# A last output tile split 384 to 128 and copied out by two engines, six more stores, and the k-v products of batch two copied out first

## The chip, the cores and the metric

One core of a Trainium2 chip. The metric is the device time of one execution in microseconds (us); a kernel's runs agree within some tenths of a us here, and all runs compared below are of the fast state (granted TensorE clock 0.996 to 1.000 in the profiled ones). Runs of one call stand beside runs of the kernel before on the same chip.

## The reference, cut to what matters

```python
    # attention: q, k, v of shape (8, 8, 576, 64), float32
    def phi(x, c, s):
        r = np.maximum(x, 0.0)
        return np.concatenate([r * c, r * s], axis=-1)
    q_p = phi(q, cos_w, sin_w)
    k_p = phi(k, cos_w, sin_w)
    kv = np.einsum('bhsf,bhsd->bhfd', k_p, v)
    z = np.sum(k_p, axis=2)
    num = np.einsum('bhsf,bhfd->bhsd', q_p, kv)
    den = np.einsum('bhsf,bhf->bhs', q_p, z)[..., None] + 1e-06
    return (num / den).astype(np.float32)
    # ... cut: the result, as x of 4608 tokens x 512, goes into the feed-forward layer, d_ff = 1536
    g = x @ w_gate
    silu = g * (1.0 / (1.0 + np.exp(-g)))
    val = x @ w_val
    return (silu * val @ w_out).astype(np.float32)
```

The products of the feed-forward layer (L513 and L549 in the profile) carry 86% of the chain that ended last.

## The kernel before

Everything is scheduled by hand: engines run their instructions in the order in which the program names them, and a framework inserts the semaphore waits. TensorE writes its products to PSUM ("banks" in the profile); ScalarE and VectorE copy them out of it, and SyncE issues most of the stores. The parts that matter are the copies of batch two's k-v products and of its turned (transposed) q from PSUM, and the output tiles.

```python
def qturn_pe(b, j, lo, hi, eng):          # transposes of q on TensorE, then one copy ("phit")
    ps = take(1)...
    for c in range(lo, hi):
        nc.tensor.transpose(out=ps[:, c - lo], in_=st["qp"][:, b, c, j], identity=ident)   # L274
    copy_op(eng, qt_of(b)[...], ps[...])                                                   # L333

def kv_out(b, engs=("act", "dve"), js=slice(0, J)):     # four copies ("kvd"), two per engine
    ps = st[b, "kvps"]
    for e, eng in enumerate(engs):                      # e: one bank per engine
        for i in range(2):
            (nc.scalar.copy if eng == "act" else nc.vector.tensor_copy)(out=kvd[b % 2]..., in_=ps[hs, e, ...])  # L297
# ... cuts ...
def ffn_out(t, f0=0, f1=None):            # one tile of 128 rows x 512 columns
    ...                                   # 12 products into one bank (L549)
    ob = obp.tile([P, d_model], FP32, name="ob")
    (nc.scalar.copy if t % 2 == 0 else nc.vector.tensor_copy)(out=ob, in_=ps)
    for e in range(2):
        idx = 2 * t + e
        nc.sync.dma_start(out=out_v[idx // NC, idx % NC], in_=ob[e * SH:(e + 1) * SH])

def ffn_out_last(t):                      # the last tile, in two column parts
    for lo, hi in ((0, 320), (320, d_model)):
        ps = take(1)[:, 0:hi - lo]
        for fc in range(FC):
            nc.tensor.matmul(out=ps, lhsT=hts[tg % 2][:, fc, r:r + P], rhs=wo_sb[:, fc, lo:hi], ...)   # L568
        ob = obp.tile([P, d_model], FP32, name="ob")
        nc.scalar.copy(out=ob[:, 0:hi - lo], in_=ps)                                                    # L571
        for e in range(2):
            idx = 2 * t + e
            (nc.sync if e else nc.scalar).dma_start(out=out_v[...][:, lo:hi], in_=ob[e * SH:(e + 1) * SH, 0:hi - lo])
# ... cuts ...
at("b11", lambda: kv_mm(1), q_(1, 0, 0), q_(1, 1, 0, "dve"), lambda: kv_out(1))
```

Stores issued by SyncE and ScalarE take eight completion counters in turn, 0 to 7. At the end of the program SyncE waits for the counters one by one, in the order 0 to 7.

Of the kernel before, what the change touches and what calls it, by code (L numbers as in the profile page):

```python
# [18 lines left out]
def kernel(  # L19
# [10 lines left out]
    nc = tc.nc  # L30
# [4 lines left out]
    SH = 64  # L35
    NC = S // SH
    d_model, d_ff = moe_w_gate.shape
# [4 lines left out]
    NH = B * NC  # L42
# [23 lines left out]
    def take(n, hold=None):  # L66

        taken = {x for r in held.values() for x in r}
        free = [b for b in range(0, 8, n) if not any(b <= x < b + n for x in taken)]

        b0 = min(free, key=lambda b: (n == 1 and hold is not None and hold[0] == "o" and b ^ 1 not in taken,
                                      sorted(used[b:b + n], reverse=True)))
        if hold is not None:
            held[hold] = range(b0, b0 + n)
        touch(range(b0, b0 + n))
        return banks[:, b0] if n == 1 else banks[:, b0:b0 + n]
# [6 lines left out]
    def give_back(hold):  # L83
        touch(held.pop(hold))
# [64 lines left out]
    def idle_products(n, cols=P):  # L149
# [37 lines left out]
        out=tab.rearrange("p c e d -> p (c e) d"),  # L187
        in_=csk.rearrange("p c e -> p (c e)").to_broadcast([P, NC * 2, D]),
# [74 lines left out]
    def relu_slots(b, lo, hi, js=slice(0, J), eng="dve"):  # L263

        if "qp" not in st:
            both = rel.tile([P, G, NC, 2, D], BF16, name="r_q").rearrange("p g c w d -> p (g c w d)")
            st["qp"] = both.rearrange("p (b c j x) -> p b c j x", b=2, c=NC, j=J)
        relu_op(eng, st["qp"][:, b, lo:hi, js].rearrange("p c j (i d) -> p c (j i) d", i=2),
                raws[b, "q"][:, 2 * js.start:2 * js.stop, lo:hi].rearrange("p g c d -> p c g d"))

    def qturn_pe(b, j, lo, hi, eng):
        ps = take(1).bitcast(BF16).rearrange("p (c x) -> p c x", x=P)
        for c in range(lo, hi):
            nc.tensor.transpose(out=ps[:, c - lo], in_=st["qp"][:, b, c, j], identity=ident)  # L274
        copy_op(eng, qt_of(b)[:, :, j, lo:hi].rearrange("p e c s -> p c e s"),
                ps[:, 0:hi - lo].rearrange("p c (e s) -> p c e s", e=2))

    def kv_mm(b):
        ps = st[b, "kvps"] = take(2, ("kv", b))
        for j, c in [(j, c) for j in range(J) for c in range(NC)]:  # L280
            for i in range(2):
                for e in range(2):
                    es = slice(e * SH, (e + 1) * SH)
                    g = 2 * j + i
                    nc.tensor.matmul(  # L285
                        out=ps[i * D:(i + 1) * D, e, j * 2 * D1:(j + 1) * 2 * D1],
                        lhsT=raws[b, "k"][es, g, c],
                        rhs=v2s[b % 2][es, g, c, :, 0:D1],
                        start=(c == 0), stop=(c == NC - 1),
                    )  # L290

    def kv_out(b, engs=("act", "dve"), js=slice(0, J)):
        ps = st[b, "kvps"]
        for e, eng in enumerate(engs):
            for i in range(2):
                hs = slice(i * D, (i + 1) * D)
                (nc.scalar.copy if eng == "act" else nc.vector.tensor_copy)(  # L297
                    out=kvd[b % 2][hs, e, js, :, i].rearrange("p j w x -> p (j w) x"),
                    in_=ps[hs, e, js.start * 2 * D1:js.stop * 2 * D1].rearrange("p (y x) -> p y x", x=D1))
# [10 lines left out]
    def kv_free(b):  # L310
        give_back(("kv", b))
# [226 lines left out]
    out_v = out.rearrange("(b p c) f -> b c p f", p=SH, c=NC)  # L538
    o_ps = {}

    def ffn_out(t, f0=0, f1=None):

        f1 = FC if f1 is None else f1
        if f0 == 0:
            o_ps[t] = take(1, ("o", t))
        tg, i = divmod(t, GH // 2)
        r = i * P
        for fc in range(f0, f1):
            nc.tensor.matmul(out=o_ps[t], lhsT=hts[tg % 2][:, fc, r:r + P], rhs=wo_sb[:, fc],  # L549
                             start=(fc == 0), stop=(fc == FC - 1))  # L550
        if f1 < FC:
            return
        ps = o_ps.pop(t)
        give_back(("o", t))
        ob = obp.tile([P, d_model], FP32, name="ob")
        (nc.scalar.copy if t % 2 == 0 else nc.vector.tensor_copy)(out=ob, in_=ps)  # L556
        for e in range(2):
            idx = 2 * t + e
            nc.sync.dma_start(out=out_v[idx // NC, idx % NC], in_=ob[e * SH:(e + 1) * SH])

    def ffn_out_last(t):

        tg, i = divmod(t, GH // 2)
        r = i * P
        for lo, hi in ((0, 320), (320, d_model)):
            ps = take(1)[:, 0:hi - lo]
            for fc in range(FC):
                nc.tensor.matmul(out=ps, lhsT=hts[tg % 2][:, fc, r:r + P], rhs=wo_sb[:, fc, lo:hi],  # L568
                                 start=(fc == 0), stop=(fc == FC - 1))
            ob = obp.tile([P, d_model], FP32, name="ob")  # L570
            nc.scalar.copy(out=ob[:, 0:hi - lo], in_=ps)  # L571
            for e in range(2):
                idx = 2 * t + e
                (nc.sync if e else nc.scalar).dma_start(out=out_v[idx // NC, idx % NC][:, lo:hi],
                                                        in_=ob[e * SH:(e + 1) * SH, 0:hi - lo])


# [29 lines left out]
    def at(s, *fns):  # L607
        plan.setdefault(s, []).extend(fns)
# [5 lines left out]
    def a_(t, j):  # L614
        return lambda: (a_half(t, j), x_norm(t) if j else None)
# [4 lines left out]
    def q_(b, j, part, eng="act"):  # L620
        lo, hi = ((0, CUT), (CUT, NC))[part]
        return lambda: qturn_pe(b, j, lo, hi, eng)
# [72 lines left out]
    for g, s in enumerate(("b9", "b9", "b10", "b10")):  # L695
        at(s, lambda g=g: vmul(1, g))
    at("b10", lambda: relu_slots(1, 0, CUT, slice(0, 1), "act"), lambda: relu_slots(1, 0, CUT, slice(1, 2)))
    at("b11", lambda: kv_mm(1), q_(1, 0, 0), q_(1, 1, 0, "dve"), lambda: kv_out(1))
    at((0, 0), lambda: kv_free(1), a_(4, 0), a_(4, 1))
    at((0, 2), a_(5, 0))  # L700
    at((0, 3), a_(5, 1))
# [21 lines left out]
    for i, (piece, t) in enumerate(steps0):  # L723
        ffn_out(t, 4 * piece, 4 * piece + 4)
        slot(divmod(i, 4))
# [38 lines left out]
    for t in range(2 * OUT, NTG * OUT):  # L764
        tg, i = divmod(t, OUT)
# [12 lines left out]
    for tg in range(1, NTG):  # L778
        s0 = SLOTS * tg
        for fc in range(FC):  # L780
            ffn_fc(tg, fc)
            slot(s0 + fc)
        for i in range(OUT):
            if tg == NTG - 1 and i == OUT - 1:
                ffn_out_last(tg * OUT + i)
            else:
                ffn_out(tg * OUT + i)
            slot(s0 + FC + i)
# [31 lines left out]
```

## Time and profile before

| what | value |
|---|---|
| median of 3 runs | 325.12 us (324.85 to 325.15) |
| span in the profile | 323.2 us |
| TensorE busy | 316.1 us, 98% |
| last product's end to the end of the span (the "tail" below) | 3.985 us |
| batch two's first k-v product to the return to the output products | 4.139 us |

A line of the chain of waits has a start, a duration and what the chain passed through. In a line of groups or of the timeline stand the engine, the source line of the kernel, the operation, its output and inputs, and the number of elements; "[1.04 <-PE banks L568]" is idle time before it and what ended it.

### The profile page before, as it was taken

To read this page: it belongs to the slowest core of one execution; us is meant where nothing else is said; L and a number is where in the kernel's file an instruction comes from. 1 tells how busy PE (TensorE), PEld (TensorE's weight loads), DVE (VectorE), ACT (ScalarE), POOL (GpSimd) and SP (SyncE) were. 2 spreads that over 40 slices of the span, in tenths; PEclk is the share of its full clock that TensorE was granted. 3 is DMA by queue.
4 is the path that set the end of the run, shared out by engine and by line. 5 is a ranking of instruction groups with operands and counts; after the bars stand their busy time and mean duration, and the time that the engine had idled before them with its cause. 6 is when DMAs were issued, how large, how long until landed. Compare 5 with 4: busy or idle time off the path is not lost.

```text
span 323.2 us, 6031 instructions
## 1 busy us (share of the span) xinstructions
PE 316.1 (98%) x2384; PEld 159.0 (49%) x2384; DVE 180.9 (56%) x363; ACT 130.7 (40%) x239; POOL 35.3 (11%) x60
## 2 busy tenths in 40 slices
PE   7899999999999999999999999999999999999995
PEld 3596555454445444544454445444544444444443
DVE  7873766787448747564756555755573236323320
ACT  7553546662436345333533354335432132213311
POOL 6755002010101000110011000200000000000000
PEclk9999999999999999999999999999999999999999
DMA  7999997987995988599679968895912401240014
GB/s 267 215 200 197 206 194 136 213 113 108 178 200 79 184 152 134 79 175 177 116 97 160 164 123 118 134 184 109 134 36 48 103 14 35 50 103 11 0 32 97
DMA packets 74379, 41.01 MB, mean 127 GB/s; under 512 B 49904, under 2 KB 69104, under 8 KB 74352
## 3 DMA queue, kind: packets, MB, share of 16 engines
q1 hardware_dynamic: 52000, 22.95, 38.9%
q0 software_dynamic: 22192, 17.57, 36.6%
q8 instruction: 18, 0.29, 0.4%
q10 hardware_dynamic: 160, 0.13, 0.1%
q14 instruction: 9, 0.07, 0.1%
HBM read 37.75 MB, written 9.44 MB: 146 GB/s over the span
## 4 chain that ended last, share of the span: by engine, by line
PE 95%; ACT 2%; DVE 2%; issue 0%; ACTq 0%
PE banks L513 58%; PE banks L549 28%; PE banks L285 3%; PE banks L399 2%; PE banks L444 1%; PE banks L381 1%; DVE v L239 1%; PE banks L152 1%; PE banks L568 1%; PE banks L325 0%; PE banks L485 0%; ACT L184 0%; ACT phit L333 0%; PE banks L274 0%; ACT ob L571 0%; DVE qwT L369 0%
## 5 line engine op out<-in xcount | busy, mean ns | idle before, releaser
L524 DVE TENSOR_TENSOR ht<-sg,banks 128x512 bf16<-128x512 bf16 (+2 forms) x116 | 74.7, 650 | 68.7 <-PE banks L513 60.3
L513 PE MATMUL banks<-xT,wv_sb 128*128 128x512 bf16 (+2 forms) x464 | 111.3, 364 | 0.0
L513 PE MATMUL banks<-xT,wg_sb 128*128 128x512 bf16 (+2 forms) x464 | 111.3, 364 | 0.0
L519 ACT ACTIVATE sg<-banks 128x512 bf16<-128x512 f32 (+2 forms) x116 | 65.8, 568 | 111.6 <-PE banks L513 107.7
L549 PE MATMUL banks<-wo_sb,ht 128*128 128x512 bf16 x420 | 93.8, 379 | 0.0
L513 PEld LDWEIGHTS <-wv_sb 128*128 128x128 bf16 x464 | 44.8, 98 | 48.7
L513 PEld LDWEIGHTS <-wg_sb 128*128 128x128 bf16 x464 | 43.1, 98 | 42.8
L549 PEld LDWEIGHTS <-ht 128*128 128x128 bf16 x420 | 40.3, 98 | 45.7 <-issue 0.2
L556 ACT COPY ob<-banks 128x512 f32<-128x512 f32 x18 | 10.6, 586 | 54.0 <-PE banks L549 54.0
L235 DVE TENSOR_TENSOR r_q<-raw_q,tab 128x1152 bf16<-128x1152 bf16 x24 | 17.9, 754 | 20.7 <-ACT raw_q L218 20.7
L556 DVE COPY ob<-banks 128x512 f32<-128x512 f32 x17 | 11.7, 691 | 28.6 <-PE banks L549 28.6
L239 DVE TENSOR_TENSOR v<-raw_v,tab 128x1152 bf16<-128x1152 bf16 x31 | 22.8, 753 | 0.1
L421 DVE TENSOR_TENSOR x<-banks,rec 128x512 bf16<-128x512 f32 (+1 forms) x32 | 21.6, 674 | 1.3 <-PE banks L381 0.3
L218 ACT ACTIVATE raw_k<-raw_k 128x576 bf16<-128x576 bf16 (+1 forms) x25 | 17.1, 694 | 0.0
L218 ACT ACTIVATE raw_q<-raw_q 128x576 bf16<-128x576 bf16 x24 | 15.5, 679 | 0.0
L729 POOL COPY hold<-phit 1x2 bf16<-1x2 bf16 x5 | 0.9, 175 | 129.6 <-DMA phit<-r_q 129.6
L399 PEld LDWEIGHTS <-phit 128*128 128x128 bf16 (+1 forms) x240 | 10.0, 100 | 6.5 <-issue 1.3
L399 PE MATMUL banks<-kv,phit 128*128 128x65 bf16 (+1 forms) x240 | 11.6, 195 | 0.0
L152 PE MATMUL banks<-zeros 128*128 128x64 bf16 (+1 forms) x64 | 8.5, 292 | 1.0 <-DVE zeros L147 1.0
L308 DVE CAST kv<-banks 64x260 bf16<-64x260 f32 x12 | 5.1, 428 | 7.4 <-ACT kv L308 7.3
L285 PEld LDWEIGHTS <-raw_k 64*64 64x64 bf16 x504 | 7.6, 106 | 3.0 <-issue 2.1
L285 PE MATMUL banks<-v,raw_k 64*64 64x130 bf16 x504 | 8.8, 218 | 0.0
(84 smaller groups left out, 130.9 us busy)
## 6 DMA issues: line engine op xcount, KB each, us to landing
out_dram<-ob SPq DMA_DIRECT2D x70, 128.0 KB, 2.4
raw_k<-in_k_dram POOLq DMA_DIRECT2D x7, 576.0 KB, 9.1
raw_q<-in_q_dram POOLq DMA_DIRECT2D x6, 576.0 KB, 6.3
raw_v<-in_v_dram POOLq DMA_DIRECT2D x6, 576.0 KB, 12.0
wo_sb<-in_moe_w_out_dram POOLq DMA_DIRECT2D x3, 512.0 KB, 13.0
wg_sb<-in_moe_w_gate_dram POOLq DMA_DIRECT2D x5, 256.0 KB, 8.6
wv_sb<-in_moe_w_val_dram POOLq DMA_DIRECT2D x5, 256.0 KB, 9.2
wo_sb<-in_v_dram SPq DMA_DIRECT2D x2, 576.0 KB, 4.3
```

What stands on the lines that cost most here:

```text
L152: nc.tensor.matmul(out=ps, lhsT=zeros, rhs=zeros[:, 0:cols].unsqueeze(1).to_broadcast([P, 4, cols]), start=True, stop=True)
L218: nc.scalar.activation(out=out, in_=in_, func=AF.Relu)
L235: nc.vector.tensor_tensor(out=st[b, "q"][:, g], in0=o.unsqueeze(2).to_broadcast([P, NC, 2, D]), in1=tab, op=ALU.mult)
L239: nc.vector.tensor_tensor(out=v2s[b % 2][:, g, :, :, 0:D], in0=(first if b == 0 and g == 0 else {"v": raw_of(b, "v")})["v"][:, g].unsqueez ...
L285: nc.tensor.matmul(out=ps[i * D:(i + 1) * D, e, j * 2 * D1:(j + 1) * 2 * D1], lhsT=raws[b, "k"][es, g, c], rhs=v2s[b % 2][es, g, c, :, 0:D ...
L399: nc.tensor.matmul(out=ps[ms, e, g * D1:(g + 1) * D1], lhsT=phit[b][:, e, g, c:c + n].rearrange("p c s -> p (c s)"), rhs=kv2s[b % 2][:, e, ...
L421: nc.vector.tensor_tensor(out=st["x", t].rearrange("p (y e d) -> p e y d", e=2, d=D)[:, :, ys], in0=ps[:, :, 0:2 * J * D1].rearrange("p e ...
L513: nc.tensor.matmul(out=st["f", tg, fc, lo][i], lhsT=(wg_sb, wv_sb)[i][:, kc, fs], rhs=xT[tg][:, ts, kc], start=(kc == 0), stop=(kc == KC - 1))
L519: nc.scalar.activation(out=sg[:, 0:n], in_=st["f", tg, fc, lo][0], func=AF.Silu)
L524: nc.vector.tensor_tensor(out=hts[tg % 2][:, fc, r:r + n], in0=st.pop(("s", tg, fc, lo))[:, 0:n], in1=ps[1], op=ALU.mult)
L549: nc.tensor.matmul(out=o_ps[t], lhsT=hts[tg % 2][:, fc, r:r + P], rhs=wo_sb[:, fc], start=(fc == 0), stop=(fc == FC - 1))
L556: (nc.scalar.copy if t % 2 == 0 else nc.vector.tensor_copy)(out=ob, in_=ps)
```

## The change

Its intent, as far as the diff tells: to empty the k-v products as soon as they are there; to have less left after TensorE's last product and two engines on it; and, with six more stores, to give the last stores other completion counters.

```diff
@@ ffn_out
         for e in range(2):
             idx = 2 * t + e
-            nc.sync.dma_start(out=out_v[idx // NC, idx % NC], in_=ob[e * SH:(e + 1) * SH])
+            parts = 2 if NH - 10 <= idx < NH - 4 else 1
+            for i in range(parts):
+                cols = slice(i * d_model // parts, (i + 1) * d_model // parts)
+                nc.sync.dma_start(out=out_v[idx // NC, idx % NC][:, cols], in_=ob[e * SH:(e + 1) * SH, cols])
@@ ffn_out_last
-        for lo, hi in ((0, 320), (320, d_model)):
+        for lo, hi in ((0, 384), (384, d_model)):
...
-            nc.scalar.copy(out=ob[:, 0:hi - lo], in_=ps)
+            mid = (hi - lo) // 2
+            nc.scalar.copy(out=ob[:, 0:mid], in_=ps[:, 0:mid])
+            nc.vector.tensor_copy(out=ob[:, mid:hi - lo], in_=ps[:, mid:hi - lo])
             for e in range(2):
                 idx = 2 * t + e
-                (nc.sync if e else nc.scalar).dma_start(...)
+                (nc.scalar if e else nc.sync).dma_start(...)
@@ the plan
-    at("b11", lambda: kv_mm(1), q_(1, 0, 0), q_(1, 1, 0, "dve"), lambda: kv_out(1))
+    at("b11", lambda: kv_mm(1), lambda: kv_out(1), q_(1, 0, 0), q_(1, 1, 0, "dve"))
```

More of the change, by code (lines that the diff above doesn't have):

```diff
@@ L570, in ffn_out_last @@
             ob = obp.tile([P, d_model], FP32, name="ob")
-            nc.scalar.copy(out=ob[:, 0:hi - lo], in_=ps)
+            mid = (hi - lo) // 2
+            nc.scalar.copy(out=ob[:, 0:mid], in_=ps[:, 0:mid])
+            nc.vector.tensor_copy(out=ob[:, mid:hi - lo], in_=ps[:, mid:hi - lo])
             for e in range(2):
                 idx = 2 * t + e
-                (nc.sync if e else nc.scalar).dma_start(out=out_v[idx // NC, idx % NC][:, lo:hi],
+                (nc.scalar if e else nc.sync).dma_start(out=out_v[idx // NC, idx % NC][:, lo:hi],
                                                         in_=ob[e * SH:(e + 1) * SH, 0:hi - lo])
```

## The prediction

> **What bounds the kernel now.** I read four views in this order: the page's busy shares and chain, TensorE's gaps, the chain of waits around 38 to 46 us, and the records of the last 6 us.
>
> ```profile
> PE 316.1 (98%) x2384; PEld 159.0 (49%) x2384; DVE 180.9 (56%) x363; ACT 130.7 (40%) x239; POOL 35.3 (11%) x60
> ...
> PE 95%; ACT 2%; DVE 2%; issue 0%; ACTq 0%
> ```
>
> TensorE is busy 98% of the 323.2 us and carries 95% of the chain that ended last. So time is lost or won only where TensorE stands still, and after its last product. I compared each matmul's start with that of the one before. From 43 us to 319 us nothing but steps of 0.10 us is lost, 18 of them, each where products of one size or shape give way to another. Nothing waits for a load or a transpose there, so a shift of TensorE at 43 us should arrive whole at the end. One real stop lies just ahead, in the chain between 38 and 46 us (start us, us, what):
>
> ```profile
> 38.88 1.27 PE banks L285 x69
> 40.15 0.51 PE banks L274 x7
> 40.66 0.02 issue
> 40.69 0.91 ACT phit L333
> 41.59 0.27 ACT kvd L297
> 41.87 0.01 issue
> 41.88 0.38 ACT kvd L297
> 42.26 0.04 issue
> 42.30 0.72 PE banks L444 x7
> ```
>
> Batch two's k-v products end at 40.15. ScalarE then waits for the transposes of q, copies those out (phit), and only then copies the k-v products (kvd), although these were there first. TensorE comes to the attention products (L444) at 41.83, does one, and stands until 42.30: 0.36 us beyond its pace, ended by ScalarE's second kvd copy. VectorE's second one, ending at 42.48, costs another 0.12 us at 42.53. Together 0.48 us.
>
> The other place is the end. ScalarE's timeline from 317.9 us on, and the last stores (KB each, us from issue to landing):
>
> ```profile
> 318.26 0.43 ACT L571 COPY ob<-banks 128x320 f32<-128x320 f32 x1 [1.04 <-PE banks L568]
> 318.72 0.56 ACTq L574 DMA_DIRECT2D out_dram<-ob  x1
> 319.40 0.32 ACT L571 COPY ob<-banks 128x192 f32<-128x192 f32 x1 [0.71 <-PE banks L568]
> 319.75 0.50 ACTq L574 DMA_DIRECT2D out_dram<-ob  x1
> ```
>
> ```profile
> out_dram<-ob SPq DMA_DIRECT2D x1, 48.0 KB, 1.9
> out_dram<-ob ACTq DMA_DIRECT2D x1, 48.0 KB, 2.1
> ```
>
> TensorE's last product ends at 319.22, the last copy at 319.72, the last stores are issued at 319.75, ScalarE's lands near 321.85, and the span ends at 323.2. Note the second copy: it could have begun at 319.26 (0.04 after its product, as the first did), but ScalarE was issuing a store until 319.28 and had a semaphore instruction after it.
>
> After the landing, SyncE's records show one wait after another at steps of 0.06 us, each for one of eight store counters in the fixed order 0 to 7: counter 0 is passed at 321.87, counter 7 at 322.30, the drain is at 322.37. The stores take these counters in turn. In the kernel before, ScalarE's last store is on counter 0, so seven waits still follow its landing.
>
> **What the Trainium skill says.** "PSUM — Partial Sum Buffer", section "PSUM bank collisions raise a hardware error": no two of TensorE, ScalarE and VectorE may be on the same bank and quadrant at once, two readers included, so software must order them. The trace of before agrees that such pairs are ordered. Later batches empty their k-v products with both engines out of the same banks at disjoint columns (L308), and the table of waits (us in total, times, longest) says
>
> ```profile
> DVE kv L308 <- ACT kv L308: 7.3, 6, 1.2
> ```
>
> VectorE begins each time only when ScalarE is through. "Perfetto Trace Analysis", section "DMA Instruction — HWDGE (DVE, Sync)": the shown span of a store's issue is the sequencer's; only at its end is it free for its next instruction, and the data moves outside it. It agrees: the ScalarE issue of 0.56 us is what the second copy waited out. "DMA: Bandwidth & Descriptors", section "Anatomy of one DMA", written for the GpSimd path: about 2.0 us fixed, most of it the write's receipt. These SyncE and ScalarE stores took 1.9 to 2.4 us for 48 to 128 KB, so it agrees in size. "TensorEngine Tiling (Array Packing)", "Key Properties": a change of tiling mode drains the array. The 0.10 us steps at 41.83 and 42.95, into and out of half-width weights, fit, and this change keeps them.
>
> **The change part by part.**
>
> *K-v products first.* Nothing is added; ScalarE's and VectorE's two casts each move ahead of the phit copies. ScalarE is idle from 39.35, so it starts at 40.15 + 0.04 = 40.19. Two casts at the 0.39 pace of before bring it to 40.97, and the phit copy (0.91) ends at 41.88. TensorE may go on 0.05 later, at 41.93. VectorE is busy to 40.31, then 0.85 for its casts and 0.63 for its phit copy: 41.79, before it is needed. So the first attention product starts at 41.83 to 41.93 instead of 41.83, and the others follow without a stop: of the 0.48 us, 0.43 to 0.48 is saved. I take **-0.46 us**.
>
> *384 and 128 columns.* TensorE's sum does not change. The trace's paces are 135.5 ns for 320 columns, 82.5 for 192, 216 for 512 and 55.7 for 128 columns (L274). 384 lies at 162.5. Twelve of each: 2.616 before, 2.618 after; the last product still ends at 319.22. The first part ends later, though: 316.44 + 11 x 0.1625 + 0.33 of latency = 318.56, where it was 318.23.
>
> *Both engines on one bank.* The built program has VectorE's copies wait for ScalarE's count, not for TensorE's: its half comes after ScalarE's half, as at L308. Durations: ScalarE 512 columns 586 ns, 320 426, 192 319; so 0.83 ns a column and 159 fixed, 64 columns 212. VectorE 512 columns 692; at one column per 1.04 ns (its clock from the 0.96 GHz of the skill's table is an estimate, no run here shows the slope) 158 fixed, hence 358 for 192 and 225 for 64. First part: ScalarE 318.60 to 318.91, VectorE 318.95 to 319.31. Only then can either store be issued: 319.34. ScalarE's issue takes 0.56, to 319.90, and holds back its second copy, whose product has been ready since 319.22. Two semaphore instructions follow instead of one (before: one took 0.12 from the issue's end to the copy's start), say 0.18: ScalarE 320.08 to 320.29, VectorE 320.33 to 320.55, stores 320.58. Before, these were issued at 319.75: **+0.83 us**. Their 32 KB instead of 48 land perhaps 0.05 sooner: -0.05 us.
>
> *Six more stores.* The six stores of the tiles before last go out as twelve halves. SyncE issues each in about 0.53 us, so four per tile take 2.1 us of the 2.6 us between two tiles; they are out by 316.9, before the next tile's copy is done at 317.22. Bytes stay the same. None is on the chain. What they do is turn the counters by six: the last two stores come on counters 6 (ScalarE) and 7 (SyncE). Six fewer waits at 0.062 us follow the last landing: **-0.37 us**.
>
> Sum: -0.46 + 0.83 - 0.05 - 0.37 = **-0.05 us**. From 325.12 that is 325.07; I put down 325.05.
>
> **The rivals.** First: the two engines copy at once, as the change seems to intend. Then part one is out by 318.96, ScalarE's issue ends at 319.54, its second copy at 319.93, where I have VectorE's at 320.55: the end comes some 0.6 us sooner, 324.45. Against it stand the waits in the built program and the L308 row. Second: the kernel gains at 42 us but something later takes it back, such as weights or k and v of batch three landing at fixed times. Then it is 325.5. Against it: not one matmul after 43 us waited for a transfer. Third: the twelve half stores get in the way, in SyncE's queue or on the 16 DMA engines (busy 94% from 316 to 317 us), and push the last landings by some tenths: 325.4. For it speaks only that 2.1 of 2.6 us of SyncE are full; the landings of 2.2 to 2.4 us leave room.
>
> **Range and chances.** The terms of opposite sign nearly cancel, so each one's error counts: some 0.05 us at the k-v copies, 0.15 us in the chain of copies and issues, 0.05 us in the counters. The three runs of before spread by 0.3 us. Together about 0.25 us either way, with rival one on the low side: 324.6 to 325.4. Two per cent is 6.5 us, which no rival comes near.
>
> **What would show it.** TensorE's second L444 product near 41.93, no stop before 43 us, and everything after it 0.46 us earlier. In the tail VectorE's half copies start 0.04 us after ScalarE's end, the last stores are issued some 1.36 us after the last product's end (0.53 before), and SyncE has one or two waits after the last landing instead of eight. The prediction is wrong if VectorE's copies start beside ScalarE's, if ScalarE copies while its store is being issued, or if TensorE shows a new gap after 43 us.

## More of the kernel before

SyncE's own table of waits before the change, from 319 us on (us in total, times, longest), has its waiting for the last stores in one piece:

```profile
SPq L815 <- DMA out_dram<-ob: 1.6, 1, 1.6
```

## The result, and the profile after

The changed kernel took 325.39 us in the median of four runs (325.13, 325.31, 325.48, 326.01), the kernel before 324.99 us. The ratio is 1.0015 (95% interval 0.9998 to 1.0032). Ratios are the mean time of one kernel's fast runs over the mean of the other's fast runs of the same rounds, so not quite the ratio of the medians. A later repeat with five rounds gave 325.15 against 324.80, ratio 1.0009. So the two kernels are the same at 2%, and neither interval (the second is 0.9994 to 1.0023) excludes that they are equal; the medians have the changed one 0.35 to 0.40 us slower, and the stretches of the traces below 0.32 us, where I had 0.05 us faster.

The page of the changed kernel, busy time and chain:

```profile
PE 315.8 (98%) x2374; PEld 158.9 (49%) x2384; DVE 181.8 (56%) x365; ACT 130.5 (40%) x239; POOL 35.1 (11%) x60
...
PE 94%; ACT 2%; DVE 2%; DMA 1%; issue 0%; SPq 0%; ACTq 0%
```

Ten matmul records are missing (2,374 of 2,384; the 2,384 weight loads are all there), so a short gap of 0.22 us in this trace is a lost record and not a stop. The chain now has 1% of DMA in it. That is a wait put down to the wrong cause. ScalarE's two copies of the last tile wait for several semaphores each, and the view puts both waits down to stores that were landing at that moment ("[1.36 <-DMA out_dram<-ob]" and "[1.15 ...]" below). But the first copy begins 0.02 us after its product is signalled, 0.633 us before the last product's end, where the kernel without the six stores has 0.634. And the landing named for the second is complete only 0.17 us after that copy began; what held it is ScalarE's own issue of a store.

The chain of waits of the changed kernel between 38 and 46 us:

```profile
38.72 1.28 PE banks L285 x70
40.01 0.00 ACTq L297
40.01 0.04 issue
40.05 0.38 ACT kvd L297
...
40.44 0.37 ACT kvd L297
...
40.83 0.92 ACT phit L333
41.75 0.04 issue
41.79 0.64 PE banks L444 x8
```

The kvd copies now come first and the eight attention products run through in 0.64 us. From the first k-v product to the return to the output products it is 3.704 us, 0.435 less than before.

The timeline of the changed kernel's last 6 us, cut to ScalarE, VectorE and the last tile's stores:

```profile
317.99 0.32 ACT L576 COPY ob<-banks 128x192 f32<-128x192 f32 x1 [1.36 <-DMA out_dram<-ob]
318.35 0.36 DVE L577 COPY ob<-banks 128x192 f32<-128x192 f32 x1 [4.20 <-ACT ob L576]
318.73 1.70 SPq L580 DMA_DIRECT2D out_dram<-ob  x2
318.74 0.56 ACTq L580 DMA_DIRECT2D out_dram<-ob  x1
319.46 0.21 ACT L576 COPY ob<-banks 128x64 f32<-128x64 f32 x1 [1.15 <-DMA out_dram<-ob]
319.71 0.23 DVE L577 COPY ob<-banks 128x64 f32<-128x64 f32 x1 [1.01 <-ACT ob L576]
319.97 0.50 ACTq L580 DMA_DIRECT2D out_dram<-ob  x1
```

VectorE's half begins each time when ScalarE's half is done (318.35 after 318.31; 319.71 after 319.68). ScalarE's second copy begins at 319.46, 0.84 us after its last product (318.63), because the issue of its first store ran to 319.29. The last stores and SyncE's waits for them (KB and us to landing; us in total, times, longest):

```profile
out_dram<-ob SPq DMA_DIRECT2D x1, 32.0 KB, 1.8
out_dram<-ob ACTq DMA_DIRECT2D x1, 32.0 KB, 2.0
```

```profile
SPq L821 <- DMA out_dram<-ob: 1.1, 2, 0.8
```

The wait for landings now ends late in the row of counters and not at its start. I cut each trace at three marks: the first k-v product of batch two, the last product's end, and the last landing. The differences between the marks add up to the span:

| stretch, us | before | changed | difference |
|---|---|---|---|
| start to first k-v product | 38.815 | 38.653 | -0.16 |
| k-v products, copies, attention | 4.139 | 3.704 | -0.435 |
| from there to the last product's end | 276.265 | 276.270 | +0.005 |
| to the issue of ScalarE's last store | 0.527 | 1.339 | +0.81 |
| its issue to its landing | 2.104 | 2.039 | -0.065 |
| landing to the end of the span | 1.354 | 1.358 | +0.004 |
| span | 323.204 | 323.363 | +0.16 |

The first row is chance: the change touches nothing there, and over the 14 traces it lies between 38.55 and 38.95. This wander is as large as the scatter of most run times. The surprise is the row from landing to end. It was to be 0.37 us shorter.

### The profile page after: what moved, and what is told of

Read it like the earlier page. It is cut to its first block, busy times and chain, and to the rows that moved or that the text cites. A ratio compares the mean times of both kernels' runs of the same rounds, so it can differ in the third digit from the quotient of the medians.

```text
span 323.4 us, 6039 instructions
## 1 busy us (share of the span) xinstructions
PE 315.8 (98%) x2374; PEld 158.9 (49%) x2384; DVE 181.8 (56%) x365; ACT 130.5 (40%) x239; POOL 35.1 (11%) x60
## 4 chain that ended last, share of the span: by engine, by line
PE 94%; ACT 2%; DVE 2%; DMA 1%; issue 0%; SPq 0%; ACTq 0%
PE banks L513 58%; PE banks L549 28%; PE banks L285 3%; PE banks L399 2%; PE banks L444 1%; PE banks L381 1%; DMA out_dram<-ob 1%; DVE v L239 1%; PE banks L152 1%; PE banks L325 0%; PE banks L485 0%; ACT L184 0%; ACT phit L333 0%; ACT kvd L297 0%; DVE qwT L369 0%
```

## The experiments

In the single records of SyncE the changed kernel passes counter 6 (ScalarE's landing) at 322.02 us and counter 7 only at 322.41, although SyncE's store on counter 7 had landed at 321.73. A step of 0.06 had become one of 0.39. Theory 1: the count of waits is what matters and the step is chance. Theory 2: the step belongs to a fixed place of SyncE's instruction stream, to which the six added stores have moved the end waits.

### The k-v copies alone

```diff
-    at("b11", lambda: kv_mm(1), q_(1, 0, 0), q_(1, 1, 0, "dve"), lambda: kv_out(1))
+    at("b11", lambda: kv_mm(1), lambda: kv_out(1), q_(1, 0, 0), q_(1, 1, 0, "dve"))
```

> Only the k-v copies ahead of the phit copies. Both theories: TensorE's stop of 0.48 us at 42 us goes and the end comes 0.42 us sooner (the size it had in the changed kernel's trace), time ratio about 0.9987. If the start of the kernel also differs by 0.16 us, as between the two traces, that is chance and not of this edit.

Measured: 324.42 us against 324.82, ratio 0.9983 (0.9970 to 0.9996). The stretch from the first k-v product is 3.710 us, 0.43 less, and the tail 3.993, as before. This part is worth 0.43 us and keeps it to the end.

### The last tile alone

The changed `ffn_out_last` with the stores of the other tiles and the plan as before.

> Only the last tile: 384 and 128 columns, both engines, the swapped queues. VectorE's half after ScalarE's; last stores issued 0.80 us later against the last product than before; the wait order at the end as before (counters 0 and 1, seven or six waits after). Expected +0.75 us, ratio about 1.0023. Rival (both engines at once): +0.2 us or less.

Measured: 325.47 against 324.82, ratio 1.0016 (1.0004 to 1.0028). The tail is 4.642 us, 0.66 more. I had expected +0.75: the last stores were issued 0.75 us later, not 0.80, landed 0.075 us sooner, and the stretch behind the landing was 0.02 us shorter. The table of waits of this run shows the order of the two engines (the total also holds VectorE's idle time of 4.2 us before the first half):

```profile
DVE ob L577 <- ACT ob L576: 5.1, 2, 4.2
```

### The six stores alone

```diff
+            parts = 2 if NH - 10 <= idx < NH - 4 else 1     # and the loop over the parts
```

> Only the six more stores; the last stores fall on counters 6 and 7. Theory 1 (only the number of waits after the last landing counts, and the 0.39 us step before SyncE's last counter in the changed kernel's trace was chance): 0.35 to 0.40 us sooner, ratio 0.9988. Theory 2 (the step belongs to the six more instructions of SyncE, for example to where its instruction stream stands, and is there in every run): step of 0.39 us before the last counter's wait again, time within 0.1 us of before.

Measured: 324.94 against 324.82, ratio 0.9999 (0.9987 to 1.0011). The tail is 4.059 us, 0.07 more. The step is there again, 0.37 us between counters 6 and 7, so theory 1 falls: not chance, and not of the changed tail.

### The changed kernel without the six stores

```diff
-            parts = 2 if NH - 10 <= idx < NH - 4 else 1
+            parts = 1
```

> The changed kernel without the six more stores: -0.42 for k-v, +0.80 for the tail, seven waits after the last landing. Theory 1: +0.35 us against before, and 0.35 slower than the changed kernel would be without its step. Theory 2: +0.35 us against before, as the changed kernel itself was (+0.13 in the profiled run, +0.4 in the medians).

Measured: 325.12 against 324.82, ratio 1.0021 (0.9993 to 1.0049; one of six runs took 328.26 and spoils the mean). The stretches: k-v 3.705, tail 4.652, as in the parts measured alone. No step; the eight waits go by in steps of 0.06. This is the time of the changed kernel with its six stores, within 0.1 us: the six stores bring nothing.

### Fourteen and seven more stores

If the place in the stream matters, moving it must move the step. Fourteen stores keep the counters (fourteen is six plus eight) and put every end wait eight places later; seven move both by one.

```diff
-            parts = 2 if NH - 10 <= idx < NH - 4 else 1
+            parts = 2 if NH - 18 <= idx < NH - 4 else 1     # fourteen; NH - 11 for seven
```

The diff is against the kernel with the six stores alone.

> Before, with fourteen more stores in place of six: the last stores fall on counters 6 and 7 again, but everything in SyncE's instruction stream stands eight places later. Position theory: the step of 0.37 us before SyncE's ninth end wait (seen in the changed kernel and with six stores alone) goes, and the kernel is 0.3 us faster than with six stores, 0.25 to 0.3 us faster than before. Rival (the step belongs to a wait that comes right behind a long one late in the list, wherever the stream stands): step of 0.37 again, time as with six stores, within 0.1 us of before.

> Before, with seven more stores: ScalarE's last store on counter 7, SyncE's on counter 0, so the wait for ScalarE's landing is the last of the nine. Position theory (a fixed place of the stream): the place moves by one, to the instruction before the ninth wait, and is hidden by the wait for the landing; 0.35 to 0.4 us faster than before. Rival (the instruction behind the long late wait is the slow one): the drain behind the ninth wait comes 0.37 us after it; time within 0.1 us of before.

Measured: fourteen 324.71 us, seven 325.00, before 324.83; ratios 0.9995 (0.9982 to 1.0008) and 1.0004 (0.9991 to 1.0018). The tails are 3.724 and 4.204 us, where before has 3.985; so fourteen gain the expected 0.26 us in the tail, but only 0.12 in the medians, which is not clear of noise. SyncE's records, in us after the last product's end, read from the traces one by one; a star marks a wait that a landing ended, an arrow the step:

```
                 before  changed   six    seven  fourteen
first wait        1.04    1.85     1.09    1.09  > 1.39
counter 0         2.65*   1.91     1.16    2.46*   1.48
counter 1         2.72    1.97     1.23    2.52    1.55
counter 2         2.78    2.04     1.29    2.59    1.62
counter 3         2.84    2.12     1.38    2.67    1.68
counter 4         2.90    2.51*    1.80*   2.75    1.83*
counter 5         2.96    2.58     1.87    2.82    1.89
counter 6         3.02    3.40*    2.73* > 3.21    2.78*
counter 7         3.08  > 3.78   > 3.11    3.29    2.84
drain             3.15    3.87     3.19    3.36    2.91
end of the span   3.98    4.74     4.06    4.20    3.72
record with step   -       207      207     207     207
```

The step stands before record 207 of SyncE, counted from 0, in all of these programs, whatever that record waits for: the ninth end wait with six stores, the eighth with seven, the first with fourteen, where it is over long before the landing. The program of before ends at record 206. The same step is in every one of the 14 traces before record 79, which is 128 records earlier: 0.44 to 0.46 us between a transpose's issue and the next semaphore instruction, where the other 34 such pairs of a trace have 0.06 or less. The pages' table of queues has a matching sign (packets, MB, share), before and changed:

```profile
q14 instruction: 9, 0.07, 0.1%
```

```profile
q14 instruction: 10, 0.08, 0.1%
```

One more packet on an instruction queue lies within the span in every kernel whose SyncE reaches record 207 (six, seven, fourteen, changed, and those below with them), and in none of the others; it has 8,192 bytes and comes 0.6 to 1.0 us after the step. In the others a packet of this size comes 0.96 to 1.21 us after the end of the span. The packet begins only when the step is over (after record 79 the next one comes 1.3 to 3.7 us later), so the step is not a wait for this packet. "Runtime: NRT & Kernel Launch", section "Instruction fetch mechanics", says that an engine refills its instruction memory in blocks over a DMA queue of its own, and that the cost of crossing a block is mostly hidden. "Perfetto Trace Analysis", section "The 4-stage abstract model", gives an instruction 64 bytes, so by an estimate 128 of them are the 8,192 bytes of the packet. That the step is a crossing of such a block fits the distance of 128 records, but is not shown; shown is only that it is tied to the place in the stream, not what SyncE does in it.

My expectation for seven stores was wrong in its time. The step moved by one place as position demands, but SyncE's own store had come to counter 0, at the head of the row. Its landing (2.44 us) was then followed by seven waits and the step.

### Columns only, and the queues only

```diff
-        for lo, hi in ((0, 320), (320, d_model)):      # first kernel
+        for lo, hi in ((0, 384), (384, d_model)):
-                (nc.sync if e else nc.scalar).dma_start(...)   # second kernel
+                (nc.scalar if e else nc.sync).dma_start(...)
```

> Before, with 384 and 128 columns but ScalarE alone copying and the old queues. Worked from the traces: ScalarE's 384-column copy ends 0.39 us later than the 320-column one, its store issue holds its second copy until 0.56 us after the last product's end, the last stores are issued 0.80 us after it (before 0.53; both engines 1.28). So the column split alone costs +0.27 us less 0.05 to 0.09 for the smaller last stores: +0.2 us; the rest of the +0.66 us of the tail alone, some 0.45 us, is the second engine's. Rival (the split of columns is free and all is the second engine's): +0.0.

> Before with the two queues of the last tile's stores exchanged and nothing else. ScalarE's last store, which lands 0.25 us after SyncE's, moves from counter 0 to counter 1: one wait less behind it, -0.06 us at most; so the +0.43 us that the changed tail has beyond its columns (0.66 less 0.23) is that of the second engine's copies. Rival: the exchange itself costs some tenths.

Measured: columns only 325.02 against 324.83, ratio 1.0006 (0.9994 to 1.0019), tail 4.210 us; queues only 324.94 against 324.80, ratio 1.0001 (0.9986 to 1.0015), tail 3.975. So of the 0.66 us that the last tile costs, the column split has 0.23 and the queues -0.01. The rest, 0.44, is left to the second engine by subtraction; both engines with 320 and 192 columns were not run.

### Another last tile: one engine for each part

k-v copies first, 352 and 160 columns, ScalarE copying the first part and VectorE the second, each from its own bank; queues as before.

```diff
-        for lo, hi in ((0, 320), (320, d_model)):
+        for lo, hi in ((0, 352), (352, d_model)):
-            nc.scalar.copy(out=ob[:, 0:hi - lo], in_=ps)
+            copy_op("dve" if lo else "act", ob[:, 0:hi - lo], ps)
```

> k-v copies first, and in the last tile 352 and 160 columns with ScalarE copying the first part and VectorE alone the second, each from its own bank, stores as before. If ScalarE's store issue and not the copy holds the second part, VectorE starts its copy 0.04 us after the last product, the last stores are issued 0.38 to 0.42 us after it instead of 0.53, and the kernel gains 0.10 to 0.2 us beyond the 0.40 of the k-v copies: 0.5 to 0.6 us faster than before. Rival (the copy's place does not matter because the issue units are busy until then): 0.4 us, as with the k-v copies alone.

Measured: 324.43 against 324.83, ratio 0.9990 (0.9978 to 1.0003). The medians alone would not tell it from the k-v copies alone, but this trace is one of those with a late start (38.82), and its five times fall in two groups (324.34 to 324.43, and 324.82 and 324.84). Its k-v stretch is 3.706 and its tail 3.867, 0.12 less than before. The timeline of its end:

```profile
317.99 0.45 ACT L333 COPY ob<-banks 128x352 f32<-128x352 f32 x1 [1.20 <-PE banks L568]
318.47 1.23 SPq L574 DMA_DIRECT2D out_dram<-ob  x2
318.48 1.40 ACTq L574 DMA_DIRECT2D out_dram<-ob  x2
318.88 0.33 DVE L333 COPY ob<-banks 128x160 f32<-128x160 f32 x1 [4.57 <-DMA out_dram<-ob]
```

VectorE begins its copy (318.88 to 319.21) while ScalarE is still issuing its first store (318.48 to 319.04), 0.09 us after the last product's end at 318.79; I had expected 0.04. The last stores are issued at 0.45 us after it, where before has 0.53.

### The changed kernel again, and with fourteen stores

> The changed kernel as it is, with five rounds. From the parts measured alone: k-v copies -0.43, last tile +0.66, six stores +0.07: +0.30 us against before. Position theory: the record number 207 of SyncE (counted from 0) is again the wait for counter 7, 0.36 us behind the wait for counter 6. If the runs of 325.5 to 326.0 seen once with this kernel are its own, they come again; if chance, all stay near 325.1.

> The changed kernel with fourteen more stores in place of six: the last stores on counters 6 and 7 as in the changed kernel, record 207 of SyncE now the first of the end waits, long before the landing. Position theory: 0.33 us faster than the changed kernel (as between fourteen and six alone: ends 3.72 and 4.06 us after the last product), so about the time of before, -0.03 us; this is what the prediction had said of the changed kernel. Rival (the step comes with any late wait of the changed tail): as the changed kernel, +0.30 us.

Measured: the changed kernel 325.15, with fourteen stores 324.91, before 324.80; ratios 1.0009 (0.9994 to 1.0023) and 1.0000 (0.9986 to 1.0015). Their tails are 4.741 and 4.413 us, 0.33 apart as expected, with equal issue times of the last stores (1.344 and 1.340); ScalarE's took 0.07 us longer to land with fourteen (2.111 against 2.039). From landing to end it is 1.358 and 0.962 us. Before has 1.354 there. So the stretch is 0.39 us shorter once the step is out of the way, where the prediction had 0.37, and by its stretches the kernel is then where the prediction had put the changed one (k-v -0.43, tail +0.43); its median is 0.11 above before's, within the scatter of the starts. The 326.01 us did not come again (325.04 to 325.45 here).

### What works, together

k-v copies first, one engine for each part, and fourteen more stores.

> k-v copies first (-0.43 us), VectorE alone copying a last part of 160 columns (-0.12), fourteen more stores (-0.26 alone, of which 0.05 for a second semaphore instruction before ScalarE's second copy that is not in the way here, so up to -0.31): 0.8 us faster than before if the three add up, 324.0 us. Rival (the tail's parts cover each other): 0.5 us.

Measured: 324.00 us against 324.80 (ratio 0.9975, 0.9960 to 0.9989), the fastest of all and clear of noise. Its tail is 3.524 us, 0.46 less than before. Its profiled run was the slowest of its five (324.30), and shows why: the load of w_out came late, and the k-v stretch was 4.116 us in it. From the table of waits of that run:

```profile
PE banks L549 <- DMA wo_sb<-in_moe_w_out_dram: 0.4, 1, 0.4
```

So the arrival of w_out may be the next bound at 41 us; why it was late is not known. In the other six traces with the k-v copies first it was in time.

## Why the prediction was wrong

- **k-v copies first: right.** -0.46 us predicted, -0.43 measured, alone and in the changed kernel; all of it arrived at the end. The rival that something later takes it back holds only for a run such as the profiled one of the combined kernel.
- **Both engines on one bank: right in mechanism and size.** VectorE's halves began 0.03 us after ScalarE's ended. The last stores were issued 0.81 us later, predicted 0.83. That the first store's issue holds ScalarE's second copy is shown by the kernel that gave this copy to VectorE. The rival of two engines at once fell. VectorE's pace, for which the prediction had no run, came out as assumed: 692, 358 and 225 ns for 512, 192 and 64 columns are 1.04 ns a column.
- **Smaller last stores: right.** -0.05 predicted, -0.065 measured.
- **Six more stores: this is the step that failed.** The prediction said "Six fewer waits at 0.062 us follow the last landing: -0.37 us". The counters turned as it said and one wait followed ScalarE's landing. But the six stores are also six more instructions of SyncE, and they moved its stop before record 207 to a place behind the last landing, where it costs. Instead of seven waits of 0.06 there was one of 0.39; the term measured +0.004, with all the rest of the stretch. The trace of before showed such a stop at record 79, hidden among waits; I had not looked for it, and I took every step of SyncE to be 0.06.
- **The sum.** -0.43 + 0.81 - 0.065 + 0.00 is +0.32 us, and 325.12 + 0.32 is 325.44 (325.31 from the 324.99 of before's four runs), against 325.39 measured. With -0.37 in place of the 0.00 it would be -0.06, as predicted. The range gave this term 0.05 us, too little for one that took all of SyncE's steps to be equal without having looked at each.

The third rival, half stores in the way of the last landings, also fell: they landed in 2.1 us, and the last ones in 1.8 and 2.0. With six stores alone ScalarE's second copy begins 0.06 us later than before, because it has a second semaphore instruction in front; that is a real but small cost of the stores.

What stays open is what SyncE does during the step, and why one run of the changed kernel took 326.01 us and one of the kernel without the six stores 328.26 (with a granted clock of 0.992, the lowest of all runs).

## What to carry to other kernels

In these runs two engines that emptied one PSUM bank did so one after the other, 0.03 us apart, and ScalarE began no copy during the 0.50 to 0.64 us in which it issued a store. At the end of a kernel, then, give each part of the last tile its own bank and its own engine, and let an engine that has no store to issue copy the last one. When instructions are added to shift something at the very end, look at each engine's single records and not only at the groups: a stop that is tied to a place in the stream cost nothing here among waits and 0.33 us behind the last landing. Where a prediction is a sum of terms that nearly cancel, the range must be as wide as the least certain of them.

## What the Trainium skill lacked or had wrong

- "Runtime: NRT & Kernel Launch", "Instruction fetch mechanics": it speaks of blocks of 16 KiB and 256 instructions and of a cost that is mostly hidden. Here SyncE stops 128 records apart (gaps of 0.44 to 0.46 us before record 79 and 0.35 to 0.36 before record 207, where 0.03 to 0.06 is usual), and the packets of one instruction queue have 8,192 bytes; those of the other (18 packets) have 16,384. Among waits the stop cost nothing; behind the last landing it cost 0.33 us (tails of 4.741 and 4.413 us). That the stop is a fetch is not shown.
- No page was found to tell how the end of a program waits for the store counters: one after another, 0.06 us each, in a fixed order, so that the place of the last store's counter, with no stop in the way, is worth 0.39 us (1.354 and 0.962 us from landing to end).
- "PSUM — Partial Sum Buffer", "PSUM bank collisions raise a hardware error": its rule agrees, but it gives no time for the handover. Here 0.03 us pass between ScalarE's end and VectorE's start.
- "Perfetto Trace Analysis", "DMA Instruction — HWDGE (DVE, Sync)": it gives no duration for an issue. A store of 64 rows mostly took 0.47 us to issue on SyncE when nothing was issued just before and 0.54 to 0.61 right behind another (single ones up to 0.79), and 0.50 to 0.64 on ScalarE; 128, 192 and 512 columns made no difference to the 0.47.
